# Chunked attention and a multiplicative feed-forward on one core: fp32 start, paced loads, alternating moves and a reordered step list

## The chip, the core and the metric

The kernel runs on one core of a Trainium2 chip. The metric is the device time of one execution in microseconds; the time before is the median of three runs. A core has five engines that run their own instruction queues in order and wait for one another through semaphores: TensorE (PE; its weight loads are shown apart as PEld) multiplies matrices into PSUM, VectorE (DVE) and ScalarE (ACT) do elementwise work, GpSimd (POOL) and SyncE (SP) here only issue transfers. Sixteen DMA engines carry the transfers of all queues.

## What is computed

```
# q, k, v: (8, 8, 576, 64) float32; chunk = 64, so 9 chunks per sequence
scores = scale * np.matmul(q_c, k_c.transpose(0, 1, 2, 4, 3))   # within a chunk of 64 tokens
attn   = exp(scores - max) / sum
out    = np.matmul(attn, v_c)                                   # (B, H, S, D)
x      = out.transpose(0, 2, 1, 3).reshape(4608, 512)
a, b   = x @ w1, x @ w2                                         # (4608, 1024) each
h      = a * b @ w3                                             # w3: (1024, 1024)
result = h @ w_out                                              # w_out: (1024, 512), float32 result
```

## The kernel before

All operands are bf16; the loads cast them from fp32 on the way, and are therefore issued by POOL. The two last products are merged: w3 is transposed (steps V) and multiplied with w_out once (steps W, copied out by Z) into `w3o`, so that tokens need only A, B and O.

Work goes by pairs `p` = 0 to 17, of 256 tokens (four chunks) and all 8 heads. Two pairs make a group `g`. For a pair the steps are:

- `q`, `k`, `v`: loads. `qk` has 5 buffers, so that a load of pair p waits for the transposes of pair p-5; `vbuf` has 6, waited for through P. A pair that crosses a sequence's end is loaded in more pieces (7 transfers instead of 4).
- `T` (DVE): transposes q (`T p.0`) and k (`T p.1`) in blocks of 32 into `qkT`.
- `G` (SP, from pair 8 on): eight transfers of 128 KB within SBUF per group, which put the 32-row blocks of `qkT` together into `qkm` so that S can use 64 rows.
- `S` (PE): scores into PSUM; `E` (ACT): exponential; `P` (PE): product with v, whose extra column of ones gives the sums, into two PSUM buffers; `N` (DVE): reciprocal and scaling, one per PSUM buffer; `X` (DVE): transposes into `xt` (or into `xm`, from where `H`, eight transfers by SP per group, fills `xt`).
- `A p.j`, `B p.j` (PE): a slice of the tokens times a slice of w1 and of w2 into the two halves of one PSUM buffer; `C` (ACT) copies the A half to SBUF, `M` (DVE) multiplies it with the B half into `ab`. Pairs 0 to 3 go alone (8 matmuls of 256 columns per step), later pairs two at a time under the even number (4 matmuls of 512 columns).
- `O` (PE): `ab` times `w3o`, 16 matmuls of 512 columns; `Y` (ACT) copies the result to `o_sb` (2 buffers); `Q` (SP) stores 512 KB. The last pair's O copies and stores in three pieces itself.

Weights are loaded by POOL in quarters: `i j` holds the columns of w1 and w2 that A and B with j (pairs 0 to 3) need; `o` is w_out, `h0` and `h1` the halves of w3 that V0 to V3 and V4 to V7 need. `D` issues matmuls on zeros.

The order is written out: `ORDER` (line 9 on) is a list of steps that the last lines of the kernel go through, and every instruction is kept in program order on its engine. All PSUM tiles share one rotation of four buffers (S one, P two, A/B one, O one, W one), so a step that takes a buffer waits for the reader of the tile four places before it: M for A and B, E for S, N for P, Y for O. POOL has eight loads in flight: each load waits for the eighth before it. The first two pairs are loaded, transposed, multiplied and exponentiated in halves of the heads (`q0.0`, `T0.0.0`, `S0.0`, `E0.0`, `P0.0`). The start and the end of the list are:

```
q0.0 k0.0 q0.1 k0.1 v0 q1.0 q1.1 k1.0 k1.1 i0 v1 q2 k2 i1 v2 i2 i3 q3 k3 v3 o h0 h1 q4 k4 v4
D0.0.32.64 T0.0.0 T0.1.0 T0.0.1 S0.0 T0.1.1 q5 k5 v5 E0.0 S0.1 E0.1 P0.0 P0.1 T1.0.0 N0.0 T1.1.0
...
M16.4 B16.5 C16.5 A16.6 M16.5 B16.6 C16.6 A16.7 M16.6 B16.7 C16.7 O13 M16.7 O14 Y13 Q13 O15 Y14 Q14
O16 Y15 Q15 O17 Y16 Q16 Y17 Q17
```

Of the kernel before, what the change touches and what calls it, by code (L numbers as in the profile page):

```python
# [7 lines left out]

ORDER = """
q0.0 k0.0 q0.1 k0.1 v0 q1.0 q1.1 k1.0 k1.1 i0 v1 q2 k2 i1 v2 i2 i3 q3 k3 v3 o h0 h1 q4 k4 v4  # L10
D0.0.32.64 T0.0.0 T0.1.0 T0.0.1 S0.0 T0.1.1 q5 k5 v5 E0.0 S0.1 E0.1 P0.0 P0.1 T1.0.0 N0.0 T1.1.0
T1.0.1 S1.0 T1.1.1 q6 k6 v6 E1.0 X0.0 S1.1 N0.1 X0.1 P1.0 E1.1 T2.0 A0.0 T2.1 q7 k7 B0.0 C0.0 P1.1
v7 M0.0 A0.1 N1.0 B0.1 C0.1 X1.0 S2 N1.1 E2 M0.1 X1.1 P2 A1.0 N2.0 B1.0 X2.0 C1.0 A1.1 N2.1 B1.1
M1.0 C1.1 X2.1 A2.0 M1.1 B2.0 C2.0 A2.1 M2.0 B2.1 T3.0 C2.1 A0.2 M2.1 B0.2 C0.2 T3.1 q8 k8 v8 A1.2
M0.2 B1.2 C1.2 S3 M1.2 A2.2 E3 B2.2 C2.2 P3 M2.2 A0.3 N3.0 B0.3 X3.0 C0.3 A1.3 N3.1 B1.3 M0.3 C1.3
X3.1 A2.3 M1.3 B2.3 C2.3 A3.0 M2.3 B3.0 V0 C3.0 A3.1 M3.0 B3.1 V1 C3.1 A3.2 M3.1 B3.2 C3.2 V2 A3.3
M3.2 B3.3 C3.3 V3 W0 M3.3 T4.0 W1 Z0 V4 V5 T4.1 q9 k9 v9 W2 Z1 V6 V7 T5.0 S4 Z2 W3 T5.1 q10 k10 E4
T6.0 T6.1 P4 v10 q11 k11 Z3 S5 N4.0 O0 E5 X4.0 N4.1 X4.1 T7.0 O1 T7.1 Y0 Q0 T8.0 P5 v11 q12 k12 Y1
S6 T8.1 O2 Q1 E6 N5.0 X5.0 N5.1 X5.1 O3 T9.0 T9.1 Y2 G4.0 P6 v12 q13 k13 A4.0 N6.0 B4.0 G4.1 Y3 X6.0
N6.1 C4.0 A4.1 X6.1 B4.1 C4.1 M4.0 Q2 S7 Q3 M4.1 A4.2 E7 T10.0 B4.2 C4.2 T10.1 P7 v13 q14 k14 A4.3  # L20
M4.2 B4.3 N7.0 C4.3 A4.4 X7.0 M4.3 B4.4 C4.4 N7.1 A4.5 M4.4 B4.5 C4.5 X7.1 S8 M4.5 S9 E8 A4.6 T11.0
B4.6 E9 T11.1 P8 v14 q15 k15 C4.6 A4.7 M4.6 G5.0 B4.7 C4.7 N8.0 A6.0 M4.7 B6.0 N8.1 C6.0 G5.1 A6.1
X8.0 B6.1 M6.0 C6.1 X8.1 P9 v15 q16 k16 A6.2 M6.1 N9.0 B6.2 C6.2 N9.1 A6.3 M6.2 B6.3 C6.3 X9.0 A6.4
M6.3 B6.4 C6.4 X9.1 A6.5 T12.0 H4.0 B6.5 C6.5 M6.4 A6.6 M6.5 B6.6 T12.1 H4.1 C6.6 S10 S11 M6.6 E10
A6.7 T13.0 B6.7 E11 P10 v16 q17 k17 T13.1 C6.7 O4 M6.7 G6.0 N10.0 N10.1 X10.0 G6.1 P11 v17 Y4 X10.1
O5 N11.0 N11.1 Q4 X11.0 X11.1 T14.0 A8.0 H5.0 Y5 B8.0 T14.1 C8.0 A8.1 M8.0 B8.1 H5.1 C8.1 T15.0 A8.2
B8.2 M8.1 C8.2 T15.1 Q5 A8.3 B8.3 C8.3 M8.2 G7.0 S12 M8.3 S13 E12 A8.4 T16.0 B8.4 E13 G7.1 P12 T16.1
C8.4 A8.5 B8.5 M8.4 C8.5 N12.0 A8.6 M8.5 B8.6 C8.6 N12.1 A8.7 M8.6 B8.7 C8.7 X12.0 P13 M8.7 A10.0
X12.1 B10.0 C10.0 N13.0 A10.1 M10.0 B10.1 N13.1 C10.1 A10.2 X13.0 B10.2 M10.1 C10.2 X13.1 S14 S15
M10.2 E14 A10.3 H6.0 T17.0 B10.3 E15 P14 T17.1 C10.3 A10.4 H6.1 M10.3 B10.4 C10.4 N14.0 A10.5 M10.4  # L30
B10.5 G8.0 C10.5 N14.1 A10.6 M10.5 B10.6 C10.6 X14.0 P15 G8.1 X14.1 A10.7 M10.6 B10.7 N15.0 C10.7 O6
N15.1 M10.7 X15.0 X15.1 H7.0 S16 Y6 S17 O7 E16 E17 H7.1 P16 Y7 O8 Q6 N16.0 Q7 N16.1 X16.0 X16.1 P17
Y8 A12.0 N17.0 Q8 B12.0 N17.1 C12.0 A12.1 X17.0 B12.1 M12.0 C12.1 X17.1 A12.2 M12.1 H8.0 B12.2 C12.2
A12.3 M12.2 B12.3 C12.3 H8.1 A12.4 M12.3 B12.4 C12.4 A12.5 M12.4 B12.5 C12.5 A12.6 M12.5 B12.6 C12.6
A12.7 M12.6 B12.7 C12.7 O9 M12.7 O10 Y9 Q9 A14.0 Y10 B14.0 C14.0 Q10 A14.1 M14.0 B14.1 C14.1 A14.2
M14.1 B14.2 C14.2 A14.3 M14.2 B14.3 C14.3 A14.4 M14.3 B14.4 C14.4 A14.5 M14.4 B14.5 C14.5 A14.6
M14.5 B14.6 C14.6 A14.7 M14.6 B14.7 C14.7 O11 M14.7 O12 Y11 Q11 A16.0 Y12 B16.0 C16.0 Q12 A16.1
M16.0 B16.1 C16.1 A16.2 M16.1 B16.2 C16.2 A16.3 M16.2 B16.3 C16.3 A16.4 M16.3 B16.4 C16.4 A16.5
M16.4 B16.5 C16.5 A16.6 M16.5 B16.6 C16.6 A16.7 M16.6 B16.7 C16.7 O13 M16.7 O14 Y13 Q13 O15 Y14 Q14
O16 Y15 Q15 O17 Y16 Q16 Y17 Q17  # L40
"""


# [1 line left out]
def kernel(  # L45
# [11 lines left out]
    nc = tc.nc  # L57
    B, H, S, D = q.shape
    P = 128
    BL = 32  # L60
    NB = P // BL
    CH = 64
# [5 lines left out]
    FO = DF // P  # L68
    UT = 2 * CH
    PT = 2 * UT  # L70
    GT = 2 * PT
    NP = NT // PT
    VW = 80
    W = D + 1
    scale = 1.0 / math.sqrt(D)

    bf = mybir.dt.bfloat16
# [10 lines left out]
    def inorder(ins):  # L88
        tc.keep_in_program_order(ins)
        return ins  # L90

    def mm(*a, **kw):
        return inorder(nc.tensor.matmul(*a, **kw))  # L93

    def load(dst, src):
        return inorder(nc.gpsimd.dma_start(dst, src))  # L96

    def psum(name):
        return ps.tile([P, 2, 512], f32, tag="p", name=name)
# [8 lines left out]

    zero = consts.tile([P, 512], bf, name="zero")
    inorder(nc.vector.memset(zero[:], 0.0))  # L110
    vbuf = [consts.tile([P, 2, H, VW], bf, name=f"vbuf{i}") for i in range(6)]
    for t in vbuf:
        inorder(nc.vector.memset(t[:, :, :, D:W], 1.0))

# [11 lines left out]
    qk_t = {}  # L126

    HH = H // 2

    def heads(h):  # L130
        return slice(0, H) if h is None else slice(h * HH, (h + 1) * HH)

    def load_qk(p, which, h=None):
        if p not in qk_t:
            qk_t[p] = io.tile([P, 2, H, 2 * D], bf, tag="qk", bufs=5, name="qk")
        for s in which:
            for at, b, c, m in spans(4 * p, 4):
                load(qk_t[p][at * BL:(at + m) * BL, s, heads(h)],
                     (q, k)[s][b, heads(h), c * CH:(c + m) * CH, :].rearrange("h (p t) d -> p h (t d)", t=2))

    def load_v(p):
        for u in range(2):
            for at, b, c, m in spans(4 * p + 2 * u, 2):
                load(vbuf[p % 6][at * CH:(at + m) * CH, u, :, 0:D],
                     v[b, :, c * CH:(c + m) * CH, :].rearrange("h p d -> p h d"))

    def load_w(dst, ap, n0, n1):
        load(dst[:, :, n0:n1], ap.rearrange("(p o) n -> p o n", p=P)[:, :, n0:n1])
# [19 lines left out]
    def move(dst, src):  # L168
        inorder(nc.sync.dma_start(dst, src))
# [11 lines left out]
    def do_G(g, a):  # L181

        if a == 0:
            qkm_t[g] = asb.tile([P, 2, 2, 2, H, CH], bf, tag="qkm", bufs=2, name="qkm")
        for i in (2 * a, 2 * a + 1):
            for e in range(2):
                move(qkm_t[g][blk[2 * a + e], i % 2], qkT_t[g][blk[i], e])

    def do_S(p, hh=None):
        g, m = divmod(p, 2)  # L190
# [22 lines left out]
    def do_P(p, hh=None):  # L213


        e = e_t[p]
        for u in range(2):
            if (p, u) not in pv_t:
                pv_t[p, u] = psum("pv")
            pv = pv_t[p, u]  # L220
            for m in range(4):
                if p < 8:
                    for g in range(NB) if hh is None else (2 * hh, 2 * hh + 1):
                        for r in range(2):
                            mm(pv[blk[g], r, m * W:(m + 1) * W],
                               lhsT=e[half[r], u, 2 * g + m % 2, m // 2 * BL:(m // 2 + 1) * BL],
                               rhs=vbuf[p % 6][half[r], u, 2 * g + m % 2, 0:W], start=True, stop=True)
                else:
                    for g, r in ((0, 0), (1, 1), (1, 0), (0, 1)):
                        mm(pv[half[g], r, m * W:(m + 1) * W], lhsT=e[half[r], u, 4 * g + m, :],  # L230
                           rhs=vbuf[p % 6][half[r], u, 4 * g + m, 0:W], start=True, stop=True)

    def do_N(p, u):
        pv = pv_t.pop((p, u))[:, :, 0:4 * W].rearrange("p r (m w) -> p r m w", w=W)
# [29 lines left out]
    def do_H(g, a):  # L264

        xt = new_xt(g)[:].rearrange("p (s c) -> p s c", s=2)
        for k_ in range(2):
            for i in (2 * a, 2 * a + 1):
                move(xt[blk[2 * a + k_], i % 2], xm_t[g][blk[i], k_].rearrange("p o m t -> p (o m t)"))

    ab_t, ps_t, a_t, o_t = {}, {}, {}, {}

    def do_D(which, p, n, cols):

        d, key = (s_t, p) if which == 0 else (ps_t, (p, 0))
        if key not in d:
            d[key] = psum("z_ps")
        for _ in range(n):
            mm(d[key][:, 0, 0:cols], lhsT=zero[:, 0:P], rhs=zero[:, 0:cols], start=True, stop=True)

    def do_AB(p, j, f, which):

# [25 lines left out]
    def do_M(p, j):  # L308
        g = p // 2
        if g not in ab_t:  # L310
            ab_t[g] = msb.tile([P, FO, GT], bf, tag="ab", bufs=3, name="ab")
        if p < 4:
            o = ab_t[g][:, 2 * j:2 * j + 2, p % 2 * PT:(p % 2 + 1) * PT]
            view = lambda t: t.rearrange("p (j t) -> p j t", j=2)
        elif p < 8:
            o = ab_t[g][:, j]
            view = lambda t: t
        else:
            o = ab_t[g][:, j].rearrange("p (c s y) -> p s c y", s=2, y=BL)
            view = lambda t: t.rearrange("p (s c y) -> p s c y", s=2, y=BL)  # L320
        inorder(nc.vector.tensor_mul(o, view(a_t.pop((p, j))[:]), view(ps_t.pop((p, j))[:, 1, :])))  # L321
# [66 lines left out]
    def load_half3(i):  # L388
# [5 lines left out]

    do = {"q": load_q, "k": load_k, "v": load_v, "i": load_w12, "o": load_wo, "h": load_half3, "T": do_T, "S": do_S, "E": do_E, "G": do_G, "H": do_H,
          "P": do_P, "N": do_N, "X": do_X, "A": do_A, "B": do_B, "C": do_C, "M": do_M, "D": do_D, "V": do_V,
          "W": do_W, "Z": do_Z, "O": do_O, "Y": do_Y, "Q": do_Q}
    for step in ORDER.split():  # L400
# [31 lines left out]
```

The softmax here doesn't subtract the row's maximum and nothing guards it: scores larger than these inputs give would overflow.

## Time and profile before

| | us |
|---|---|
| runs | 249.81, 251.22, 251.6 (median 251.22) |
| the profiled execution | 251.03 |
| its span | 249.3 |
| PE busy | 226.9 (91%) |
| DVE busy | 154.5 (62%) |
| POOL busy (issuing loads) | 86.9 (35%) |
| ACT busy | 83.4 (33%) |
| PE idle before 37 us | 15.0 |
| PE idle from 240 us to the end | 5.0 |

The profile is one execution, with times from the start of its span. A page gives busy times, the span in 40 slices, the chain of work that ended last, and groups of instructions by line, engine, operation and tile; a timeline gives merged instructions in order, with the idle time before each and what ended it. Matmuls of one shape behind one another cost less than their own duration: 64 of 512 columns take 13.81 us, 216 ns each, while a single one is shown with 379 ns.

Rows of the page and of the trace that the prediction uses:

| instruction | count | mean ns |
|---|---|---|
| DVE transpose T, 128x1024 | 32 | 1290 |
| DVE transpose T, 128x512 (half) | 8 | 733 |
| DVE product M, 128x512 | 72 | 679 |
| DVE N: reciprocal and scaling | 36 each | 192 and 692 |
| DVE transpose X | 36 | 697 to 707 |
| DVE transpose V | 8 | 1220 |
| ACT copy C, 128x512 | 72 | 585 |
| ACT copy Y, 128x1024 | 17 | 1012 |
| POOL issue of a load | 112 | 581 to 934 |

Times from issue to landing, medians: loads of q and k in whole pieces 8.3 and 10.1 us, of v 8.7, of weights 10.0; moves G 7.2, moves H 3.0, stores 2.9.

### The profile page before, as it was taken

The numbers are of one execution on the slowest core, as the hardware profiler recorded it, in microseconds if no ns is written. First come the engines' busy times: TensorE is split into PE (matmuls) and PEld (weight loads), VectorE is DVE, ScalarE is ACT, GpSimd is POOL, SyncE is SP. The second block draws the span as 40 slices with busy tenths as digits, with TensorE's granted clock in tenths as the row PEclk, the third lists the DMA queues.
The fourth block names the chain that finished last, engine by engine and source line by source line (L and its number), as shares of the span: only waits on it lengthen the run. The fifth ranks groups of instructions, "written<-read, shape, count | busy, mean of one in ns | idle before, by whom it ended". The sixth has DMA issues, their size and how long they took to land.

```text
span 249.3 us, 6372 instructions
## 1 busy us (share of the span) xinstructions
PE 226.9 (91%) x2740; PEld 122.0 (49%) x2760; DVE 154.5 (62%) x236; ACT 83.4 (33%) x116; POOL 86.9 (35%) x116
## 2 busy tenths in 40 slices
PE   3328899999999999999999999999999999999992
PEld 2225688874455445444444444444444444444441
DVE  2566965899879588999998798918440331233000
ACT  2110324332343333535335325262332332331322
POOL 8977854486997254573660000000000000000000
PEclk9999999999999999999999999999999999999998
DMA  7999999999999999999999974635502200400334
GB/s 67 145 165 182 193 185 201 196 174 172 155 169 209 221 225 249 177 209 193 204 194 235 271 128 99 147 76 199 151 3 84 84 0 9 162 0 1 139 116 168
DMA packets 93660, 37.12 MB, mean 149 GB/s; under 512 B 77120, under 2 KB 86592, under 8 KB 93632
## 3 DMA queue, kind: packets, MB, share of 16 engines
q0 software_dynamic: 84736, 19.41, 84.6%
q1 hardware_dynamic: 8896, 17.31, 24.0%
q8 instruction: 22, 0.36, 0.6%
q14 instruction: 6, 0.05, 0.1%
HBM read 38.80 MB, written 9.44 MB: 194 GB/s over the span
## 4 chain that ended last, share of the span: by engine, by line
PE 73%; DMA 17%; POOL 3%; DVE 2%; issue 1%; ACT 1%; SPq 0%; DVEq 0%; ACTq 0%; POOLq 0%
PE ab_ps L93 41%; PE o_ps L93 22%; DMA out_dram<-o_sb 6%; DMA w<-in_moe_w_dram 6%; PE w_ps L93 6%; DMA qkm<-qkT 5%; PE s_ps L93 3%; PE pv L93 2%; POOL qk L96 2%; DVE qkT L177 1%; POOL vbuf L96 1%; ACT e L209 0%; DVE ab L321 0%; POOL w L96 0%; ACT a_sb L306 0%
## 5 line engine op out<-in xcount | busy, mean ns | idle before, releaser
L93 PE MATMUL ab_ps<-xt,w 128*128 128x512 bf16 (+1 forms) x697 | 130.0, 343 | 1.1 <-DMA w<-in_moe_w_dram 0.5
L93 PEld LDWEIGHTS <-w 128*128 128x128 bf16 x704 | 67.8, 99 | 55.6 <-DMA w<-in_moe_w_dram 0.9
L321 DVE TENSOR_TENSOR ab<-a_sb,ab_ps 128x512 bf16<-128x512 f32 x72 | 48.9, 679 | 49.3 <-ACT a_sb L306 49.2
L306 ACT COPY a_sb<-ab_ps 128x512 f32<-128x512 f32 x72 | 42.2, 585 | 87.9 <-PE ab_ps L93 85.9
L93 PE MATMUL o_ps<-w3o,ab 128*128 128x512 bf16 (+1 forms) x285 | 63.3, 373 | 0.6
L177 DVE STREAM_TRANSPOSE qkT<-qk 128x1024 bf16<-128x1024 bf16 (+1 forms) x40 | 45.6, 1178 | 11.0 <-DMA qk<-in_q_dram 8.3
L93 PEld LDWEIGHTS <-ab 128*128 128x128 bf16 x296 | 28.5, 98 | 32.2
L96 POOL DMA_DIRECT2D vbuf<-in_v_dram x40 | 33.8, 854 | 14.6 <-DMA qk<-in_q_dram 6.4
L351 ACT COPY o_sb<-o_ps 128x1024 f32<-128x1024 f32 x17 | 17.2, 1012 | 42.8 <-PE o_ps L93 38.8
L239 DVE TENSOR_TENSOR xn<-pv,rc 128x512 bf16<-128x512 f32 x36 | 24.9, 692 | 1.2
L96 POOL DMA_DIRECT2D qk<-in_k_dram x26 | 20.2, 782 | 10.0 <-DMA vbuf<-in_v_dram 7.3
L96 POOL DMA_DIRECT2D qk<-in_q_dram x26 | 20.3, 788 | 8.2 <-DMA qk<-in_k_dram 2.3
L209 ACT ACTIVATE e<-s_ps 128x1024 bf16<-128x1024 f32 (+1 forms) x18 | 17.1, 978 | 8.9 <-PE s_ps L93 8.7
L93 PE MATMUL pv<-vbuf,e 64*32 64x65 bf16 (+1 forms) x832 | 11.0, 200 | 4.5 <-DMA vbuf<-in_v_dram 3.3
L93 PE MATMUL w_ps<-wo,w3T 128*128 128x512 bf16 x62 | 14.0, 379 | 0.1
L93 PEld LDWEIGHTS <-e 64*32 64x32 bf16 (+1 forms) x832 | 8.3, 99 | 11.5 <-issue 6.6
L236 DVE RECIPROCAL rc<-pv 128x8 f32<-128x8 f32 x36 | 6.9, 192 | 11.3 <-PE pv L93 11.2
L96 POOL DMA_DIRECT2D w<-in_moe_w_dram x16 | 11.1, 696 | 7.4 <-DMA wo<-in_moe_w_out_dram 3.4
L259 DVE STREAM_TRANSPOSE xm<-xn 128x512 bf16<-128x512 bf16 x20 | 13.6, 697 | 0.2
L251 DVE STREAM_TRANSPOSE xt<-xn 128x512 bf16<-128x512 bf16 x16 | 11.3, 707 | 0.4
L93 PEld LDWEIGHTS <-qkT 32*64 32x64 bf16 x512 | 5.8, 116 | 11.2 <-DVE qkT L177 9.2
L344 DVE COPY o_sb<-o_ps 128x256 f32<-128x256 f32 x1 | 0.4, 424 | 16.0 <-PE o_ps L93 16.0
(19 smaller groups left out, 45.4 us busy)
## 6 DMA issues: line engine op xcount, KB each, us to landing
out_dram<-o_sb SPq DMA_DIRECT2D x17, 512.0 KB, 2.9
qkm<-qkT SPq DMA_DIRECT2D x40, 128.0 KB, 7.2
vbuf<-in_v_dram POOLq DMA_DIRECT2D x32, 128.0 KB, 8.7
w<-in_moe_w_dram POOLq DMA_DIRECT2D x16, 256.0 KB, 10.0
qk<-in_q_dram POOLq DMA_DIRECT2D x10, 256.0 KB, 8.3
qk<-in_k_dram POOLq DMA_DIRECT2D x10, 256.0 KB, 10.1
xt<-xm SPq DMA_DIRECT2D x40, 64.0 KB, 3.0
qk<-in_q_dram POOLq DMA_DIRECT2D x8, 128.0 KB, 5.1
```

The source lines that it names most:

```text
L93: return inorder(nc.tensor.matmul(*a, **kw))
L96: return inorder(nc.gpsimd.dma_start(dst, src))
L177: inorder(nc.vector.transpose(qkT_t[g][:, :, p % 2, s, heads(h)].rearrange("p e h (y t) -> p h t e y", t=2), qk_t[p][:, s, heads(h)].rearr ...
L209: inorder(nc.scalar.activation(e_t[p][:, :, heads(hh)], s_t[p][:].rearrange("p u (h q) -> p u h q", q=CH)[:, :, heads(hh)], Exp, scale=sca ...
L236: inorder(nc.vector.reciprocal(rc[:], pv[:, :, :, D:W]))
L239: inorder(nc.vector.tensor_mul(xn_t[p][:, u], pv[:, :, :, 0:D], rc.to_broadcast([P, 2, 4, D])))
L251: inorder(nc.vector.transpose(new_xt(g)[:].rearrange("p (o t) -> p o t", o=KO)[:, :, t0:t0 + UT] .rearrange("p o (m y) -> p m o y", y=BL), ...
L259: inorder(nc.vector.transpose(xm_t[g][:, u, :, m].rearrange("p o (c y) -> p c o y", y=BL), xn_t[p][:].rearrange("p u r m d -> p (u r) m d" ...
L306: inorder(nc.scalar.copy(a_t[p, j][:], ps_t[p, j][:, 0, :]))
L321: inorder(nc.vector.tensor_mul(o, view(a_t.pop((p, j))[:]), view(ps_t.pop((p, j))[:, 1, :])))
L344: inorder(copy(o_sb[:, u, n0:n1], t[:, 0, 0:n1 - n0]))
L351: inorder(nc.scalar.copy(o_sb[:], ps_t.pop(p)[:]))
```

## The change

The first q comes as fp32 through the queues of SP and ACT, half the heads each (`R0`, `R1`), and ACT copies it to bf16 (`K0`, `K1`). Pairs 0 and 1 go whole like the others; the matmuls on zeros are gone from the list. From pair 8 on, a load is preceded by a small copy on POOL that reads one value of the third load before it. `G` and `H` issue their moves in the order of blocks 0, 2, 1, 3, each G step moving one of the two halves `e` per block, and `H a` reading only the `X` of `u = a`. `vbuf` has 7 buffers instead of 6, `ab` 4 instead of 3. The list of steps is another one. Its start, the part around T15.0 and its end are shown; `K` and `R` are new.

```
 ORDER = """
...
+R0 R1 k0 v0 q1 k1 v1 q2 k2 v2 i1 i0 i3 i2 q3 k3 v3 h0 o h1 q4 k4 v4 K0 K1 T0.0 T0.1 q5 k5 v5 S0 E0
+T1.0 P0 T1.1 q6 k6 v6 N0.0 S1 N0.1 E1 X0.0 P1 T2.0 X0.1 T2.1 q7 k7 v7 S2 N1.0 X1.0 A0.1 N1.1 X1.1
+B0.1 C0.1 E2 A0.0 M0.1 B0.0 C0.0 P2 M0.0 A1.0 N2.0 A1.1 N2.1 C1.0 B1.0 X2.0 C1.1 A1.2 M1.0 B1.1 C1.2
+A1.3 M1.1 B1.2 T3.0 A0.2 B1.3 T3.1 q8 k8 v8 C0.2 C1.3 B0.2 M1.3 A0.3 M1.2 B0.3 X2.1 C0.3 S3 M0.2
+A2.0 M0.3 E3 B2.0 C2.0 A2.1 V2 P3 C2.1 M2.0 B2.1 N3.0 A2.2 M2.1 B2.2 C2.2 N3.1 A2.3 X3.0 B2.3 X3.1
+C2.3 M2.2 A3.0 V0 A3.1 C3.0 B3.0 V3 C3.1 B3.1 M2.3 W1 V1 M3.0 W0 V6 V7 T4.0 W3 Z0 M3.1 V4 Z1 T4.1 q9
...
+T13.0 B6.7 C6.7 E10 O4 M6.7 T13.1 E11 T14.0 G6.0 T14.1 P11 Y4 O5 N11.0 N11.1 G6.1 T15.0 P10 v17 Y5
+A8.2 N10.0 B8.2 N10.1 C8.2 A8.1 X10.0 A8.0 X10.1 C8.1 X11.0 B8.1 C8.0 M8.2 H5.0 B8.0 M8.1 A8.3 X11.1
...
+B16.2 C16.2 Q13 A16.4 M16.2 O14 B16.4 A16.1 B16.1 C16.1 C16.4 O15 Y14 M16.4 M16.1 Q14 O16 Y15 Q15
+Y16 Q16 O17
 """
...
-    def load(dst, src):
-        return inorder(nc.gpsimd.dma_start(dst, src))
+    last = []
+    tick = consts.tile([P, 1], bf, name="tick")
+
+    def load(dst, src, paced=False):
+
+        if paced:
+            inorder(nc.gpsimd.tensor_copy(tick[0:1], last[-3]))
+        ins = inorder(nc.gpsimd.dma_start(dst, src))
+        d = dst[0:1]
+        while len(d.shape) > 2:
+            d = d[:, 0]
+        last.append(d[:, 0:1])
+        return ins
...
+    def do_R(h):
+
+        raw_t[h] = msb.tile([P, HH, 2 * D], f32, tag="o_sb", name="raw")
+        inorder((nc.sync, nc.scalar)[h].dma_start(
+            raw_t[h][:], q[0, heads(h), 0:4 * CH, :].rearrange("h (p t) d -> p h (t d)", t=2)))
+
+    def do_K(h):
+        if 0 not in qk_t:
+            qk_t[0] = io.tile([P, 2, H, 2 * D], bf, tag="qk", bufs=5, name="qk")
+        inorder(nc.scalar.copy(qk_t[0][:, 0, heads(h)], raw_t[h][:]))
...
-        for i in (2 * a, 2 * a + 1):
-            for e in range(2):
-                move(qkm_t[g][blk[2 * a + e], i % 2], qkT_t[g][blk[i], e])
+
+        for i in (0, 2, 1, 3):
+            e = (i + a) % 2
+            move(qkm_t[g][blk[i // 2 * 2 + e], i % 2], qkT_t[g][blk[i], e])
...
-        for k_ in range(2):
-            for i in (2 * a, 2 * a + 1):
-                move(xt[blk[2 * a + k_], i % 2], xm_t[g][blk[i], k_].rearrange("p o m t -> p (o m t)"))
+        for i in (0, 2, 1, 3):
+            move(xt[blk[i // 2 * 2 + a], i % 2], xm_t[g][blk[i], a].rearrange("p o m t -> p (o m t)"))
...
-            ab_t[g] = msb.tile([P, FO, GT], bf, tag="ab", bufs=3, name="ab")
+            ab_t[g] = msb.tile([P, FO, GT], bf, tag="ab", bufs=4, name="ab")
```

`load_qk` and `load_v` pass `p >= 8` as `paced`. The list before has the same steps of the kinds A, B, C, M, N, X, V, W, Z, O, G and H, in another order.

## The prediction

> **What bounds the kernel now.** I read the page first, then busy time by stretch, then TensorE's timeline of the start, the chain of waits, and the queues' timelines where the chain touches them.
>
> ```profile
> PE 226.9 (91%) x2740; PEld 122.0 (49%) x2760; DVE 154.5 (62%) x236; ACT 83.4 (33%) x116; POOL 86.9 (35%) x116
> ...
> PE   3328899999999999999999999999999999999992
> ```
>
> TensorE is full from the sixth slice to the last. So the time is (how soon the matmuls run back to back) + (a fixed amount of matmul work) + (what comes after the last matmul). By stretch (start:end, width, then busy time of PE, PEld, DVE, ACT, POOL):
>
> ```profile
> 0.00:6.00 6.00, 1.89 (x32) 1.73 (x32) 1.43 (x8) 1.28 (x1) 4.96 (x10) 1.00 0.68 66
> 6.00:12.00 6.00, 2.31 (x128) 1.84 (x128) 2.97 (x5) 1.19 (x2) 6.00 (x9) 1.00 1.70 144
> 18.00:24.00 6.00, 5.00 (x87) 3.54 (x85) 2.92 (x3) 0.58 (x1) 4.47 (x6) 1.00 1.75 183
> 30.00:37.00 7.00, 6.90 (x62) 5.71 (x61) 4.84 (x7) 2.34 (x4) 3.57 (x6) 1.00 1.77 183
> 37.00:50.00 13.00, 13.00 (x236) 11.29 (x235) 9.05 (x15) 5.01 (x8) 5.66 (x10) 1.00 1.40 198
> ```
>
> The last column is what the DMA engines move: 66, then 144, then 183 GB/s. The start is a wait for loads. TensorE's timeline names them:
>
> ```profile
> 19.48 3.28 PE L93 MATMUL ab_ps<-xt,w 128*128 128x256 bf16 x16
> 22.69 0.42 PE L93 MATMUL pv<-vbuf,e 64*32 64x65 bf16 x32
> 23.28 1.05 PE L93 MATMUL ab_ps<-xt,w 128*128 128x256 bf16 x8 [0.17 <-DMA w<-in_moe_w_dram]
> 24.65 1.05 PE L93 MATMUL ab_ps<-xt,w 128*128 128x256 bf16 x8 [0.33 <-DMA w<-in_moe_w_dram]
> ...
> 27.54 0.70 PE L93 MATMUL pv<-vbuf,e 64*32 64x65 bf16 x64 [1.21 <-ACT e L209]
> ```
>
> At 28.24 pairs 0 to 2 are through S and P, four units (a unit is one A or B step) of weights i0 and i1 are done, and nothing stops for long after it. The first 16 matmuls take 205 ns each, later ones of the same shape 112 (30 in 3.38 us), at a granted clock of 1.00 in both rows. Later waits on TensorE are few; the chain of waits shows the one that matters, and how little it costs:
>
> ```profile
> 120.27 7.03 DMA qkm<-qkT
> ...
> 143.89 4.94 DMA qkm<-qkT
> 148.83 0.14 issue
> ```
>
> S12 (0.3 us) and S14 (0.4 us) wait for moves that land 7 to 8 us after issue; once the loads are over the same moves land in 2.4 us. At 90.5 S7 stops for 0.5 us with no releaser shown. The end:
>
> ```profile
> 243.25 2.41 SPq L169 DMA_DIRECT2D out_dram<-o_sb  x4
> ...
> 243.74 1.02 ACT L351 COPY o_sb<-o_ps 128x1024 f32<-128x1024 f32 x1
> 244.40 0.42 DVE L344 COPY o_sb<-o_ps 128x256 f32<-128x256 f32 x1 [16.04 <-PE o_ps L93]
> ```
>
> Y16's 512 KB copy stands behind O17's copies, so its store is issued last (245.28), and lands 2.8 us later, at 248.1.
>
> **The change part by part.** The sum is made against the profiled run, 251.03 us (span 249.3), 0.19 under the median of 251.22. Matmuls of A, B, S, P, W and O are the same in number; only order and waits differ.
>
> *Early loads.* In order of arrival, what matters is how many bf16 MB stand ahead. Before: i0 is complete at 1.84 MB (9.72 + 7.2 = 17.0), k2 at 2.62 (14.58 + 7.7 = 22.3), i1 at 3.15 (24.6), v2 at 3.41 (20.05 + 6.2 = 26.3), the last of wo at 6.29 (32.03 + 10.2 = 42.2). After, with q0 counted at its bf16 size, i1's two halves end at 2.62 and 2.88 MB, i0's at 3.15 and 3.41, h0 at 6.29. Call g the time by which a given MB arrives earlier. From above: from 3 to 15 us about 1.7 MB land, at 0.12 to 0.16 MB per us (POOL issues one 131 KB half per 0.73 to 0.88 us without a wait), and from 18 us on it is 0.165 and more; if the gap is due to halves alone, whole pairs return 1.7 us, and q0 may run up to 0.8 ahead of POOL's first packet: g = 2.5. From below: fp32 writes 0.52 MB where bf16 wrote 0.26, 1.6 us at 0.16 MB per us, less 0.6 for the earlier start: g = -1. I take 1.0, nearer the upper end's row (issue without a wait) than the lower but not at it.
>
> The Trainium skill speaks against this part: "DMA: Bandwidth & Descriptors", section "Issuing engines are not separate DMA queues", says that transfers issued by scalar, sync or gpsimd interleave on the same 16 engines and that several issuers save only issue time. By that rule alone the doubled bytes stay in the stream, g would be about -0.5, and the sum below 250.4 instead of 248.9.
>
> *First dense work.* A0.1 starts when i1's first half is there: 22.3 - g = 21.3, and its 16 slow matmuls (with B0.1) take 3.3: 24.6. A0.0 0.9: 25.5; i0's end, 26.3 - g = 25.3, is just in time for B0.0: 26.4; P2 0.64 + 0.2 for the change of shape (from the start of the last B to S3's is 1.07 us where a unit takes 0.87): 27.2. The same steps ended at 28.24: -1.0. The removed dummies (1.9 us) and the half steps of S, E, P lie ahead of all this: S2 needs k2, which arrives with g too, and DVE's whole transposes (1.29 against 2 x 0.73) are no dearer. K0 and K1 are two ACT copies of about 0.6 (128x512, row 585 ns), with ACT idle until its first exponential; uncovered they would cost 1.2.
>
> *V2 and X3 moved up.* V2 now stands on DVE before M2.0, and needs h0: 42.2 - g = 41.2. V2 1.2 + M2.0 0.7 give 43.1; A2.2 takes M2.0's PSUM buffer, and TensorE arrives after 16 units of 0.87 plus S3 and P3 (0.84 each) at 42.8: a stall of 0.35. Behind V2 stand N3 and X3 (five to six DVE steps, to 46.9), and A3.0 wants X3.1 at 46.7: 0.25. Together +0.6, from 0 (h0 earlier) to 1.5 (h0 a load later). Start: -0.4.
>
> *Paced loads.* POOL waits before each load from pair 8 until the third before it has landed, with a small copy as the wait (a 128x1 memset takes 0.1 us). Queued behind it are only POOL's later loads; the waiters are DVE's T8 to T17. It puts 3 loads in flight instead of 8, and moves no longer queue behind 7 us of loads: S12's and S14's 0.7 us go (S7's 0.5 I leave; both ends 0 to -1.2). What it can cost is the first rival. Moves in alternating blocks: same count, same bytes; SP issues one per 0.63 us either way (8 in 5.0), and nothing in the trace shows the landing to depend on the block: 0, and at most the 0.7 already counted. The buffers (vbuf 7, ab 4) only remove waits that I see at most 2.1 us of, on POOL, off the path: 0.
>
> *Orders.* From S3 on, S and P stand in 25 places between dense work instead of 23. From the last B's weights to S or P takes 1.17 us where a unit takes 0.86: 0.3 each, +0.6; I take +0.5, since merged ones differ. DVE is busy 9.0 to 9.8 of 10 us from 100 to 130, so a late DVE step there reaches TensorE; O3 moves 16 us of matmul work later, A12 and A16 units are spread, and the order can add stalls that I price from 0 to 2.
>
> *End.* Q16 now comes before O17: Y16's copy (1.0) fits in O17's first 1.73 us of matmul, its buffer is free (Q14's store has landed). The last store is then O17's 128 KB: copy ends 244.82, issue 0.03 later, landing 1.8: 246.6 instead of 248.1, -1.5. Only a busy DMA queue could take it back; nothing else runs then.
>
> Sum: -0.4 - 0.7 + 0.5 - 1.5 = -2.1: 251.03 - 2.1 = **248.9 us**.
>
> **The rivals.**
>
> *Slower: the paced loads come late at T15.0.* By DVE steps T15.0 stands 5.9 us earlier than before (fewer N, X and M ahead of it), at about 129.75 - 5.9 - 0.4 = 123.4, and N10.0, which frees the PSUM buffer that A8.0 takes, is queued behind it. q15 landed before at 110.35 + 12.6 = 122.9. TensorE reaches A8.0 at about 129.3 (P10 has 7.3 us more matmul work before it than at 118.8), so T15.0 must start by 127.1: the point from which it decides is a landing of q15 after 127.0, then 1 us for each us. Three in flight with about 4 us each (3.4 for the first 128 KB load, on an empty queue) bring the 36 loads from q8 to q15, the first issued at about 69, by 69 + 36/3 x 4 = 117 if moves do not delay them. The moves and stores of that stretch (four stores of 0.5 MB, G4, G5, H4: 4.7 MB at SP's pace of 131 KB per 0.63 us) are 22 us more; if nothing overlapped, 139. Against it: overlap is the rule (DMA at 190 to 238 GB/s here). At a landing of 131 to 134 it costs 4 to 7 less the wins that remain: 253 to 256.
>
> *The stream gains its full 2.5.* Then TensorE starts 1.5 earlier than in the sum: 247.4.
>
> *Nothing arrives earlier.* g = -1 or new stalls of 2 us: only the end and the two waits are won: 250.9.
>
> **How the numbers follow.** One per cent of 251.22 is 2.5 us, about what a measurement of this kernel can tell from no change: faster is under 248.7, slower over 253.7. Forecast 248.9 with its own 247.6 to 250.4: 0.48 (0.18 of it under 248.7). Full stream gain, 247.4: 0.22. Nothing earlier, 250.9: 0.12. Paced loads late: 0.18, 0.14 of it over 253.7. Faster 0.18 + 0.22 = 0.40; slower 0.14; same 0.46. Range 246.5 (full gain and S7's wait) to 253.0: outside it stay some 0.18.
>
> **What would show it.** Right: the first 16 dense matmuls start near 21.3, P2 ends near 27.2; no wait for qkm moves, which land in 3 to 5 us; the last landing 1.8 us after the last issue, with a 128 KB store. Wrong: a first dense matmul after 22.5 (fp32 q in the way); TensorE idle before A2.2 or A3.0 by more than 1 us; DVE waiting over 4 us before a transpose of qk at 120 to 130, and TensorE idle at ab_ps behind it; DVE waits for qk elsewhere between 75 and 130, which would say that three in flight are too few.

## The result and the profile after

| | us |
|---|---|
| before, beside it | 251.41 (median of 4) |
| after | 268.44 (median of 4: 263.73, 266.94, 269.93, 270.85) |
| ratio | 1.056, 95% interval 1.040 to 1.071 |
| the profiled execution, its span | 270.85, 269.1 |

Two of the four executions after, 269.93 and 270.85, count as slow, and the ratio leaves them out: by it the change makes the kernel 14 us slower, by the medians 17 us.

The page of the profile after shows where at once (busy time, then the span in 40 slices of 6.7 us):

```profile
PE 228.4 (85%) x2708; PEld 121.8 (45%) x2728; DVE 152.2 (57%) x233; ACT 82.6 (31%) x116; POOL 91.0 (34%) x159
...
PE   0249999999997899699506989999999999999995
...
PEclk9999999999999999999955999999999999999999
```

TensorE does the same work (228.4 us against 226.9), but from the thirteenth slice to the twenty-fourth it has holes. The deepest lies in slices 20 to 22 (5, 0, 6), and there the granted clock (PEclk, in tenths) falls to half. Busy time by stretch of the kernel after:

```profile
65.00:170.00 105.00, 84.59 (x1220) 41.20 (x1230) 68.52 (x106) 32.20 (x45) 46.30 (x96) 0.93 1.23 155
...
130.00:140.00 10.00, 1.61 (x23) 0.60 (x20) 1.38 (x2) 1.01 (x1) 3.18 (x7) 0.71 1.39 179
140.00:150.00 10.00, 6.33 (x34) 2.46 (x35) 6.19 (x11) 1.35 (x3) 6.07 (x14) 0.61 0.97 82
```

The same stretch of the kernel before:

```profile
65.00:170.00 105.00, 102.89 (x1518) 50.11 (x1533) 87.24 (x134) 42.26 (x56) 40.35 (x50) 1.00 1.43 189
```

The first column after the width is TensorE; the last three are the granted clock, the share of the DMA engines and GB/s. TensorE is idle for 105.0 - 84.6 = 20.4 us between 65 and 170, where it was idle for 2.1: 18.3 us more. The spans of the two profiled executions differ by 19.8 (the one profiled after is the slowest of its four, so that the others must have lost less): those 18.3 and 1.5 more of busy time. What start and end win, and what is lost outside this stretch, cancels.

Which wait ends last there is told by the chain of waits of the kernel after, between the first paced load and the end of the long hole (start, length, what):

```profile
68.15 4.39 DMA qk<-in_q_dram
...
109.30 10.29 DMA vbuf<-in_v_dram
...
131.61 9.29 DMA qk<-in_k_dram
141.02 0.18 POOL tick L100
141.20 0.33 issue
...
146.59 1.31 DVE qkT L200
```

For 78 us no matmul stands in the chain, nor any work of ACT. It goes from a load to the copy that waits for it (`tick`), from there to the next load, and so on. Before, 59% of the chain from 66 to 148 was matmuls and 34% stores and moves; no load stood in it:

```profile
by line: PE ab_ps L93 29.9%; DMA out_dram<-o_sb 19.4%; PE o_ps L93 17.0%; DMA qkm<-qkT 14.6%; DVE qkT L177 4.3%; PE w_ps L93 4.3%; PE pv L93 4.0%; PE s_ps L93 3.4%; issue 2.2%; DVE ab L321 0.9%; ACT a_sb L306 0.7%; SPq L169 0.7%
```

Note the length of a link in the chain after: 4.4 to 10.3 us in these lines from issue to landing, and 0.5 behind it (0.18 for the tick, 0.33 until the next issue starts).

How that reaches TensorE is in three timelines (start, length, engine, line, operation, count, and in brackets the idle time before it with what ended it). TensorE around the long stop:

```profile
131.29 0.32 PE L92 MATMUL pv<-vbuf,e 64*64 64x65 bf16 x16
143.08 0.44 PE L92 MATMUL pv<-vbuf,e 64*64 64x65 bf16 x16 [11.47 <-DVE xn L263]
143.92 4.64 PE L92 MATMUL ab_ps<-xt,w 128*128 128x512 bf16 x12 [0.41 <-DVE xn L263]
148.75 3.63 PE L92 MATMUL ab_ps<-xt,w 128*128 128x512 bf16 x16 [0.18 <-DVE xn L263]
```

VectorE at the same time:

```profile
135.61 1.31 DVE L200 STREAM_TRANSPOSE qkT<-qk 128x1024 bf16<-128x1024 bf16 x1 [5.53 <-DMA qkm<-qkT]
140.92 1.31 DVE L200 STREAM_TRANSPOSE qkT<-qk 128x1024 bf16<-128x1024 bf16 x1 [4.01 <-DMA qk<-in_k_dram]
142.13 0.17 DVE L260 RECIPROCAL rc<-pv 128x8 f32<-128x8 f32 x1
...
146.59 1.31 DVE L200 STREAM_TRANSPOSE qkT<-qk 128x1024 bf16<-128x1024 bf16 x1 [2.72 <-DMA qk<-in_q_dram]
```

And POOL, at q14's issue and at the tick that waits for its landing:

```profile
129.22 0.87 POOL L101 DMA_DIRECT2D qk<-in_q_dram  x1 [0.24 <-issue]
...
135.71 0.18 POOL L100 COPY tick<-qk 1x1 bf16<-1x1 bf16 x1 [2.24 <-DMA qk<-in_q_dram]
```

P10 fills two PSUM buffers. TensorE stops after the first, since the second takes the buffer that N11.0 (the reciprocal at 142.13 and the product behind it) must read out. N11.0 is ready to run, but in DVE's queue it stands behind T14.0 (135.61) and T14.1 (140.92), and these wait for q14 and k14. The row for T14.0 names a move as releaser; the tick behind q14 runs at 135.71, so q14's landing is what ended that wait. q14 was issued at 129.22, where the kernel before issued it at 105.7, because POOL waits for a landing before each load. TensorE's 12 matmuls after the stop take 387 ns each (4.64 / 12), the next sixteen 227. From 143 to 149 the granted clock is 0.60, from 148 to 153 it is 1.00: the lowered clock costs another 1.9 us.

The start and the end do what they were to do. TensorE's start after:

```profile
20.04 6.01 PE L92 MATMUL ab_ps<-xt,w 128*128 128x256 bf16 x32
25.99 0.70 PE L92 MATMUL pv<-vbuf,e 64*32 64x65 bf16 x64
```

P2 ends at 26.69 instead of 28.24. At the end the last copy (0.42 us, from 265.88) is over at 266.30 and the span ends 2.8 later, where 4.5 us lay between the two before.

### The profile page after: what moved, and what is told of

Read it like the earlier page. It is cut to its first block, busy times and chain, and to the rows that moved or that the text cites. A ratio compares the mean times of both kernels' runs of the same rounds, so it can differ in the third digit from the quotient of the medians.

```text
span 269.1 us, 6377 instructions
## 1 busy us (share of the span) xinstructions
PE 228.4 (85%) x2708; PEld 121.8 (45%) x2728; DVE 152.2 (57%) x233; ACT 82.6 (31%) x116; POOL 91.0 (34%) x159
## 4 chain that ended last, share of the span: by engine, by line
PE 58%; DMA 29%; DVE 4%; POOL 3%; issue 3%; ACT 2%; POOLq 0%; SPq 0%; DVEq 0%
PE ab_ps L92 35%; DMA vbuf<-in_v_dram 16%; PE o_ps L92 15%; DMA qk<-in_k_dram 8%; PE w_ps L92 5%; DMA qk<-in_q_dram 4%; DVE qkT L200 2%; POOL qk L101 2%; PE s_ps L92 2%; ACT a_sb L329 2%; DMA qkm<-qkT 1%; DVE xn L263 1%; POOL tick L100 1%; PE pv L92 1%; POOL vbuf L101 1%
## 5 line engine op out<-in xcount | busy, mean ns | idle before, releaser
L92 PE MATMUL ab_ps<-xt,w 128*128 128x512 bf16 (+1 forms) x697 | 134.7, 348 | 6.9 <-DVE ab L344 2.6
L92 PEld LDWEIGHTS <-w 128*128 128x128 bf16 x704 | 68.9, 100 | 62.8 <-issue 9.0
L344 DVE TENSOR_TENSOR ab<-a_sb,ab_ps 128x512 bf16<-128x512 f32 x72 | 47.5, 673 | 59.8 <-ACT a_sb L329 39.9
L200 DVE STREAM_TRANSPOSE qkT<-qk 128x1024 bf16<-128x1024 bf16 x36 | 46.4, 1300 | 35.7 <-DMA qk<-in_q_dram 17.0
L92 PE MATMUL pv<-vbuf,e 64*32 64x65 bf16 (+1 forms) x832 | 10.9, 202 | 16.7 <-DVE xn L263 11.5
L233 ACT ACTIVATE e<-s_ps 128x1024 bf16<-128x1024 f32 x18 | 18.0, 1026 | 12.6 <-PE s_ps L92 12.4
L101 POOL DMA_DIRECT2D qk<-in_q_dram x23 | 17.9, 784 | 6.1 <-issue 2.0
L101 POOL DMA_DIRECT2D qk<-in_k_dram x24 | 18.9, 789 | 3.0 <-DMA wo<-in_moe_w_out_dram 1.2
L100 POOL COPY tick<-qk 1x1 bf16<-1x1 bf16 x26 | 4.6, 177 | 40.7 <-DMA qk<-in_q_dram 21.9
L92 PE MATMUL s_ps<-qkT 32*64 32x64 bf16 x512 | 6.7, 209 | 12.4 <-DVE qkT L200 11.1
L385 DVE STREAM_TRANSPOSE w3T<-w 128x1024 bf16<-128x1024 bf16 x8 | 9.7, 1226 | 2.7 <-DMA w<-in_moe_w_dram 1.8
```

Of the source, the lines that this page charges most:

```text
L100: inorder(nc.gpsimd.tensor_copy(tick[0:1], last[-3]))
L101: ins = inorder(nc.gpsimd.dma_start(dst, src))
L200: inorder(nc.vector.transpose(qkT_t[g][:, :, p % 2, s, heads(h)].rearrange("p e h (y t) -> p h t e y", t=2), qk_t[p][:, s, heads(h)].rearr ...
L233: inorder(nc.scalar.activation(e_t[p][:, :, heads(hh)], s_t[p][:].rearrange("p u (h q) -> p u h q", q=CH)[:, :, heads(hh)], Exp, scale=sca ...
L385: inorder(nc.vector.transpose(w3T_t[f][:].rearrange("p k (f y) -> p f k y", y=BL), w3[:, NB * f:NB * (f + 1), :].rearrange("p f (k x) -> p ...
```

## The experiments

**The pacing taken out, all else as changed.**

```diff
 load_qk: load(..., 
-                     p >= 8)
+                     False)
 load_v:
-                     v[...].rearrange("h p d -> p h d"), p >= 8)
+                     v[...].rearrange("h p d -> p h d"), False)
```

> The changed kernel with the pacing alone taken out: the small copies are gone, eight loads in flight as before. Theory 1 (three loads in flight are too few: q9 to q15 land late, DVE stops at the transposes, TensorE behind it): the 20 us of idle TensorE between 80 and 180 us go, and with them the cold clock after the 11.5 us stop at P10; the time falls to 246 to 250 us. Rival (the new list of steps itself, with T14, T15 and P11 before P10, makes the stop, whoever loads): over 258 us, with waits of DVE for q and k still over 10 us in total.

Measured: 250.99 (ratio to before 0.997, 0.993 to 1.001), 1 us above the first theory's range. The pacing carries the whole loss. But what is left is no gain either, although P2 ends at 25.5, 2.8 us earlier than before, and the end is the shorter one. So a second question opened: where do these gains go?

**Five in flight instead of three.**

```diff
-            inorder(nc.gpsimd.tensor_copy(tick[0:1], last[-3]))
+            inorder(nc.gpsimd.tensor_copy(tick[0:1], last[-5]))
```

> Pacing with five in flight instead of three (the copy reads the fifth load before). Theory 1, with a load's 4 to 10 us from issue to landing as the cause: rate grows with the number in flight, so most of the loss goes: 248 to 255 us. Rival (the copy on POOL and its wait cost the time, about 0.45 us per load, not the number in flight): still over 262 us.

Measured: 249.84 (0.993, 0.989 to 0.997). All 48 ticks are still there, so the copies on POOL and the waits as such cost nothing: it is the number three.

**The pacing of three alone, on the list of before.**

```diff
 (kernel before)
+            inorder(nc.gpsimd.tensor_copy(tick[0:1], last[-3]))     # from pair 8 on
```

> The kernel before with the pacing of three alone added from pair 8 on. Theory 1: k10 to k15 land 9 to 20 us later, more than the 5 to 10 us by which DVE had its transposes covered: 256 to 268 us. Rival (pacing costs only together with the new list, which wants q14 and q15 six us earlier): 250 to 254 us.

Measured: 280.8 (1.116, 1.109 to 1.124), more than the expectation reached. The loads keep the pace that they have in the kernel after (2.20 us from issue to issue against 2.16). TensorE is idle for 25.2 us from 65 to 170 instead of 20.4, in eight stops of 0.5 to 8.6 us, six of them for an M on DVE, whose waits for `qk` come to 43.3 us. So it was not the new order that made slow loads hurt: the changed kernel bears them better than the old one. Whether its list, its two more buffers or its start do that was not tried apart.

**No pacing, and the moves of G in the old order of blocks.**

```diff
-        for i in (0, 2, 1, 3):
-            e = (i + a) % 2
-            move(qkm_t[g][blk[i // 2 * 2 + e], i % 2], qkT_t[g][blk[i], e])
+        for i in (2 * a, 2 * a + 1):
+            for e in range(2):
+                move(qkm_t[g][blk[2 * a + e], i % 2], qkT_t[g][blk[i], e])
```

> As a1_unpaced, with the moves G in their old order of blocks (H as in the change). If the order of the blocks decides how fast moves land: their time from issue to landing differs by over 1 us from a1_unpaced, and S waits for it. I expect the same time as a1_unpaced within 1 us.

Measured: 251.04 (0.999, 0.995 to 1.002), beside 250.99 with alternating blocks: no difference.

**Four in flight.**

```diff
-            inorder(nc.gpsimd.tensor_copy(tick[0:1], last[-3]))
+            inorder(nc.gpsimd.tensor_copy(tick[0:1], last[-4]))
```

> The changed kernel with four loads in flight instead of three. Theory A, a load takes 5 to 6 us whatever the number in flight, so that the rate goes with that number: with three, the some 40 loads from q8 to k15 took from 69 to 146.5, 1.9 us each; with four they take 1.45 us each and k15 lands near 127, some 2 to 4 us after it is wanted: 251 to 255. Theory B, the queue's bandwidth sets the rate and a fourth load only makes each take longer: k15 lands after 140 and the time is 262 to 268.

Measured: 258.45 (1.029, 1.024 to 1.033), between the two theories. The issues of the 37 transfers from q8 to k15 (two or three for one where a pair crosses a sequence's end) tell why. The table sets them beside TensorE's idle time between 65 and 170; the pace is the time between first and last issue through 36, and pace times number is what one load holds its place for:

| in flight | first, last issue | pace | pace x number | TensorE idle 65 to 170 | time |
|---|---|---|---|---|---|
| 3 (the change) | 68.2, 145.9 | 2.16 | 6.5 | 20.4 | 268.44 |
| 4 | 66.2, 130.5 | 1.79 | 7.1 | 10.0 | 258.45 |
| 5 | 65.1, 117.3 | 1.45 | 7.3 | 3.7 | 249.84 |
| 8 (not paced) | 63.0, 104.7 | 1.16 | 9.3 | 4.4 | 250.99 |

In the last row 6.2 of POOL's 12.5 us of waits between 63 and 105 are for buffers to come free, so that there the number alone does not set the pace.

The transfers in the stretch 68 to 148, with three in flight (count, size, median us from issue to landing):

```profile
qkm<-qkT SPq DMA_DIRECT2D x24, 128.0 KB, 7.1
...
vbuf<-in_v_dram POOLq DMA_DIRECT2D x14, 128.0 KB, 6.4
...
qk<-in_k_dram POOLq DMA_DIRECT2D x5, 256.0 KB, 8.1
```

And not paced:

```profile
qkm<-qkT SPq DMA_DIRECT2D x32, 128.0 KB, 6.5
...
vbuf<-in_v_dram POOLq DMA_DIRECT2D x16, 128.0 KB, 10.4
```

A load takes 6 to 8 us with three in flight (q's 256 KB 6.0) and some 10 with eight (q's 9.7, k's 10.2): the time falls far less than the number. So fewer in flight means a slower pace, and at 2.16 us a transfer the loads fall behind what the list wants of them (the kernel before issued the same 37 transfers 1.36 apart, from 66.4 to 115.4). The moves did not gain here: 7.1 us with three loads in flight beside them, 7.2 in the same stretch of the kernel before.

**Three in flight, the transposes moved behind on DVE.**

```diff
-... T13.1 E11 T14.0 G6.0 T14.1 P11 Y4 O5 N11.0 N11.1 G6.1 T15.0 P10 v17 ...
+... T13.1 E11 G6.0 P11 Y4 O5 N11.0 N11.1 G6.1 P10 v17 ...
-... A8.4 E13 M8.3 B8.4 T15.1 ...
+... A8.4 E13 M8.3 B8.4 T14.0 T14.1 T15.0 T15.1 ...
```

> The changed kernel, three in flight, with the transposes T14.0, T14.1 and T15.0 moved behind on DVE, from ahead of N11 and N10 to just ahead of T15.1. Theory A, the 11.5 us stop in P10 is the place of these waits in DVE's queue (N11.0, which frees a PSUM buffer, stands behind them): it goes, TensorE waits at most 3 us elsewhere before 165, and 268.4 falls to 257 to 260. Theory B, the loads are behind by their rate and any place meets them: another stop of over 6 us stands at A8.4 to S14 (behind the same transposes, or for G7's moves), and the time stays at 264 to 269.

Measured: 262.87 (1.046, 1.042 to 1.050), again between. The stop in P10 is gone; TensorE's waits afterwards:

```profile
147.21 1.89 PE L92 MATMUL ab_ps<-xt,w 128*128 128x512 bf16 x8 [2.19 <-DVE ab L344]
...
156.49 5.08 PE L92 MATMUL ab_ps<-xt,w 128*128 128x512 bf16 x16 [3.22 <-DVE xn L263]
```

TensorE's idle time between 65 and 170 falls from 20.4 to 12.9. How much time the place in DVE's queue was worth stays open: all four executions (262.50 to 263.36) lie below the change's fastest, 263.73, but the ratio of 1.046 lies within the change's interval of 1.040 to 1.071. 11.5 us over before stay while the loads go three at a time (2.05 us each). So both halves of the explanation count: the rate makes the loads late and carries most of the loss, and the place decides whom a late load stops.

**Start and end by themselves.** The start: the code of the change without pacing, its list up to P2, and from there the list of before. The end: the kernel before with one edit.

```diff
-O16 Y15 Q15 O17 Y16 Q16 Y17 Q17
+O16 Y15 Q15 Y16 Q16 O17
```

> The start alone: the code of the change without pacing, with the first part of its list (to P2: q0 as fp32 by two hardware queues, whole pairs, i1 ahead of i0, no dummy matmuls), and behind P2 the list of before, unchanged. Theory A: the start gives what P2's end shows in the unpaced run (25.4 to 26.0 against 28.24), and the list of before carries most of it to the end: 248.7 to 249.4. Theory B: TensorE that arrives earlier meets the waits for moves (S12, S14, A8.0), so that less than 1 us is left: 250.4 to 251.4.

> The end alone: the kernel before with Y16 and Q16 ahead of O17, nothing else changed. Theory A (the term of the prediction): the last store is 128 KB instead of 512 KB and is issued earlier, -1.5: 249.9 (249.6 to 250.2). Theory B: O17's copies or its small stores wait behind Q16's 512 KB store in the same queue, so that nothing is won: 251.0 to 251.6.

Measured: the start alone 248.57 (0.987, 0.984 to 0.990), 2.75 us below before; the end alone 249.23 (0.991, 0.988 to 0.995), 2.1 below. Both gains are real and reach the end. The run of the start carries the other code of the change as well (seven `vbuf`, four `ab`, the new order of moves): P3 ends at 41.41 in it instead of 42.40, so 1.0 of its gain is there by then, and S12 and S14, which waited 0.7 us for moves before, do not wait. How the 2.75 divides between start and code was not tried. What swallows both gains without pacing is the new middle of the list: around the old middle they stay, 246.66 (the last run below) against 250.99.

**Where the middle loses.** With five in flight TensorE has one stop of over 1 us behind the start, before A8.2. The row names moves into qkm; H4's moves into `xt`, which A8.2 reads, land until 126.9:

```profile
127.22 6.20 PE L92 MATMUL ab_ps<-xt,w 128*128 128x512 bf16 x28 [2.20 <-DMA qkm<-qkT]
```

The queue of SP in that run, where two 512 KB stores (Q2, Q3) stand between the halves of H4:

```profile
111.62 2.41 SPq L192 DMA_DIRECT2D xt<-xm  x4
114.13 1.08 SPq L192 DMA_DIRECT2D out_dram<-o_sb  x2
115.30 5.27 SPq L192 DMA_DIRECT2D xt<-xm  x4
```

The four moves behind the stores take 5.27 us to issue, the four ahead of them 2.41. The old list issued Q2 and Q3 at 90.9, 20 us before H4. Two runs, both with five in flight, moved the stores. The first:

```diff
-... H4.0 T12.1 ... M6.4 Q2 M6.3 B6.6 C6.6 Q3 X9.1 S10 S11 M6.6 H4.1 A6.7 ...
+... H4.0 T12.1 ... M6.4 M6.3 B6.6 C6.6 X9.1 S10 S11 M6.6 H4.1 Q2 Q3 A6.7 ...
```

> The changed kernel with five loads in flight (as in the run with five) and one edit to the list: the two 512 KB stores Q2 and Q3 are issued behind the four moves of H4.1 instead of ahead of them. Theory A: with five in flight TensorE's one stop of over 1 us is the 2.2 us before A8.2, and it comes from H4.1's moves, which are issued at 115.3 to 120 because the two stores stand before them in the queue of SP; so the stop falls to under 0.5 us and the time to 247.6 to 248.3, from 249.84. Theory B: the moves are slow because of the loads that share the queue, whatever is issued before them; then the stop stays at 1.5 us or more and the time at 249.4 to 250.2.

Measured: 250.58 (0.996, 0.994 to 0.999), no gain over 249.84. Its profile is of its slowest execution (253.54); it shows where the stop went:

```profile
126.60 6.20 PE L92 MATMUL ab_ps<-xt,w 128*128 128x512 bf16 x28 [0.18 <-DMA qkm<-qkT]
...
135.02 0.93 PE L92 MATMUL s_ps<-qkm 64*64 64x64 bf16 x63 [2.08 <-DMA qkm<-qkT]
```

A8.2 no longer waits, and S12 waits 2.08 us instead: G6's moves are now the ones behind the stores. The time lies just above the second theory's 249.4 to 250.2; the mechanism is neither's. Hence the second run:

```diff
-... G4.1 N6.0 ... G5.1 E9 ... M6.4 Q2 M6.3 B6.6 C6.6 Q3 X9.1 ...
+... G4.1 Q2 N6.0 ... G5.1 Q3 E9 ... M6.4 M6.3 B6.6 C6.6 X9.1 ...
```

> The change with five in flight and the stores Q2 and Q3 issued early (behind G4.1 and G5.1), so that neither H4's nor G6's moves stand behind them. Theory A: the 2 us stop, which stood at A8.2 with the stores ahead of H4.1 and went to S12 when they stood ahead of G6, follows the stores; now it goes: 247.4 to 248.2, from 249.84. Theory B: the moves are late from the loads beside them; then a stop of 1.5 us or more stands at A8.2 or S12 again, and the time at 249.3 to 250.3.

Measured: 247.80 (0.987, 0.982 to 0.992), 2.0 below the run with five in flight by the medians and 1.5 by the ratios (0.993, 0.989 to 0.997, whose interval it still touches), as the first theory had it. The trace is clearer than the time: A8.2 and S12 follow without a stop.

```profile
125.42 6.20 PE L92 MATMUL ab_ps<-xt,w 128*128 128x512 bf16 x28 [0.18 <-DMA qkm<-qkT]
131.55 0.71 PE L92 MATMUL s_ps<-qkm 64*64 64x64 bf16 x64
```

**A version that beats both.** Start and end of the change around the old middle, with five in flight and with eight (no pacing):

> Start and end of the change, five loads in flight, and between P2 and O17 the list of before. If the new middle of the list costs what start and end win (theory A): 246.8 to 247.8, faster than both kernels and than the whole change with five in flight (249.84). If the middle is not what costs (theory B: the gains of the start are lost in any list): 249.3 to 250.2. If the old list cannot bear even five in flight: DVE waits for qk behind T9.0 and the time is over 251.

> Start and end of the change around the list of before, without pacing (eight in flight). If the two add up as they did alone (-2.75 and -2.1 against 251.3): 246.3 to 247.0. If pacing of five is what gave part of the 247.13 of the same list with five in flight: 247.6 to 248.4.

Measured: 247.13 with five (0.980, 0.977 to 0.984), 246.66 without pacing (0.982, 0.979 to 0.985). The ratios can't be told apart: pacing, even where it does no harm, wins nothing here. Either is some 4.5 us faster than before, close to the 2.75 + 2.1 of the parts. With five in flight the new middle costs 2.7 us against the old (249.84 and 247.13), and the place of the two stores is most of it; without pacing it costs 4.3, and there the stores were not moved.

## Why the prediction was wrong

**The step that failed** is the time per paced load: "Three in flight with about 4 us each (3.4 for the first 128 KB load, on an empty queue)", 36 / 3 x 4 = 48 us, which has the last load of q15 landed by 117. Because of it the sum gave the paced loads no cost, only the 0.7 us that they were to win. The runs show 6.5 us per place, 2.16 from issue to issue where the step has 1.33, and a landing of q15 at 146.5. (The transfers from q8 to q15 are 35, not 36; that is 1.3 us.) A row of the first load on an empty queue was carried to a stretch where moves and stores run beside the loads, and the tick with the way to the next issue (0.5 us and more) was left out. How much of the rest comes from the moves and stores was not tried apart. The rows at hand were the later loads' 6 to 10 us, the prediction's own 6.2, 7.2, 7.7 and 10.2; with three in flight most of that stayed (6.0 to 8.1 for whole pieces).

**The mechanism was named, and counted for too little.** It was the first rival, at 0.18. Its rule was "a landing of q15 after 127.0, then 1 us for each us", with a landing put at 131 to 134 for its price. The last of q15 lands at 146.5 in the profile after (T15.0 starts at 146.59), and the rule with that landing gives 19.5 us before the wins are taken off; the spans differ by 19.8. That these agree is luck: the rule's one stop at A8.0 did not come, the idle time lies in several stops from 80 on, and the other three executions lost less. What spoke against the rival, "overlap is the rule", is no argument against a limit on the number in flight: such a limit is there to cap the overlap. Even the paragraph's upper end, 139 "if nothing overlapped", was passed.

**The place** was another: not A8.0 behind T15.0 and N10.0, but P10 behind T14.0, T14.1 and N11.0, one pair of steps earlier. The early sign that the prediction gave held: DVE waits for qk between 75 and 130 (81.6, 84.5, 91.2 and so on), "which would say that three in flight are too few".

**The gain of pacing**, -0.7 by S12 and S14, did not come. It rested on moves landing in 3 to 5 us; in the loaded stretch they take 7.1, as before. The page's median of 5.4 over the whole run mixes these with the moves that come after the loads (only 24 of the 40 fall in that stretch, 32 before). With pacing S12 and S14 do not wait, but TensorE then comes 20 us late to them. Without it S12 waits 0.9 us and S14 not, and in the start alone, not paced either, neither waits; with five in flight around the old middle S12 waits 1.6. So these waits hang on the times of the list, not on the pacing.

**Start**, -0.4: right in sign, too small. i1's and i0's halves landed at 20.0, 21.3, 22.7 and 24.5; at the same MB the stream before stood at 22.3 (2.62 MB), 24.6 (3.15) and 26.3 (3.41), so g is 1.8 to 2.3 instead of 1.0. The first dense matmul starts at 20.04 (21.3 predicted), but all 32 of them run slowly (188 ns), so that P2 ends only 0.5 us ahead of the predicted 27.2. TensorE is busy for 12.90 of the 13 us from 37 to 50, so the two stops after V2 and X3 (+0.6) did not occur. The run of the start measured -2.75, with the other code in it. The rule of the Trainium skill that was weighed there ("DMA: Bandwidth & Descriptors", "Issuing engines are not separate DMA queues"), that several issuers save only the time of issuing, had led to an estimate of g = -0.5. The landings come 2.3 to 2.8 us ahead of that estimate. They do not show the rule wrong: whether the two hardware queues or the whole pairs brought it was not tried apart.

**End**, -1.5: right. From the last copy to the end of the span it is 2.8 us instead of 4.5, and the end alone measured -2.1 (interval -1.3 to -3.0).

**Orders**, +0.5 with stalls from 0 to 2: right in kind, at the upper end. The stop before A8.2 costs 1.5 to 2.0, by the run that removes it. The prediction read the list for S and P between dense work and for DVE's load, and did not go through SP's queue, where the stores had moved ahead of H4.1.

**Moves in alternating blocks**, 0: right (250.99 against 251.04). The seventh `vbuf` and fourth `ab` were not tried by themselves.

## What to carry to other kernels

With a fixed number of transfers in flight, the pace is about (landing time + time to the next issue) / number, here (6.0 + 0.5) / 3 = 2.2 us: take the landing time from the loaded stretch itself, and set the sum against the time at which the list needs the last of them. A wait that is late on an in-order engine costs what stands behind it, so look for the PSUM reader behind it, and follow the place that a moved store gets in its queue. Try the parts of a bundle alone: here two parts were worth 4.5 us, and two others, the pacing and the new middle of the list, hid them.

## What the runs showed of the hardware that was not expected

- Fewer loads in flight did not reliably make the transfers beside them quicker. Moves of 128 KB landed in 7.1 us with three (5.6 with the transposes behind, 7.0 on the list of before), 6.4 with four, 5.8 with five, and 6.5 without pacing (7.2 before): two lists differ by as much as two numbers.
- A stop of TensorE costs more than its length once it is long enough. After stops of 3.22 us (three in flight, transposes behind) and 3.91 (the list of before, paced) the next 16 matmuls took 5.08 and 5.03 us instead of 3.6, with a granted clock of 0.72 in the 6 us around each; after 8.64 eleven took 4.85 (441 ns each), after 11.5 twelve took 4.64. After stops of 2.64 and 2.71 they took 3.61 and 3.63, the usual time, at 1.00.
- Shorter stops close together can do the same: after 2.50 and 0.41 us with 0.43 of work between them (four in flight) twelve matmuls took 3.96 us instead of 2.76, at a granted clock of 0.72 from 128 to 134.
